# A gated attention and MLP mix on one Trainium2 core: the last product of the second half in seven parts, and three weight quarters copied in DRAM

## The chip, the cores and the metric

The kernel runs on one core of a Trainium2 chip. The time is device microseconds of one execution; three runs of the kernel before are given. A profiled execution gives the trace: TensorE is called PE (its weight loads PEld), VectorE DVE, ScalarE ACT, GpSimd POOL, SyncE SP. SP and POOL issue nearly all DMAs.

## What is computed

The input x has 2048 rows of 1024. Two branches are mixed by a gate (cut from the reference):

```
g = sigmoid((x * gate_w).sum(-1, keepdims=True))
a = attention(x, wqkv) @ wo              # 32 heads of 32, each position sees 8 positions at a step of 2 backwards
b = (gelu(x @ w_gate) * (x @ w_up)) @ w_down     # inner width 3584
out = g * a + (1 - g) * b
```

Both output products are one in the kernel: the attention's result (1024 wide, already scaled by g) and h = gelu(..)*(..) (3584 wide) stand side by side, 4608 wide, and w_down and wo stand below each other. That "down" product, 2048 x 4608 times 4608 x 1024, is what the change touches.

## The kernel before

**The first 513 us.** The projections of x run as units of 28 matmuls of 128x512 (about 6.05 us each, lines 340 to 410); unit numbers run from 0 to 77, and functions hung on a unit with `at(unit, fn)` are issued when it begins. Beside the units, VectorE does the attention and the sums that the units need. Each pair of columns of w_gate and w_up is loaded by SP (L166, `load_pair`) some three units before use, and summed by VectorE (L322). Results go to DRAM: h (`h_d`, L259), the attention's result (`o_d`, L774), both issued by POOL. Units 36 to 53 (`NQKV + 10` is 36), of which the change speaks, run from about 263 to 372 us.

**The down product.** It runs in two halves of 1024 rows, `down(0)` and `down(1)`. Within a half, the left matrix A and the right matrix R are cut in 2x2 quarters, and the product is done with seven products of quarters and sums (a Strassen-Winograd scheme). A quarter is [128, 18, 512]: 18 slices of 128 of the inner dimension (`NK`), 512 columns. The seven products, in the order in which they run: A11·R11, A12·R21, S·T1, S2·T2 (S2 = A21 + A22 - A11), AD·T3, A22·T4, and last A12·R22, where A12 has become A12 - S2. Here these are products 1, 2, 5, 6, 7, 4 and "the last". The sums T1 to T4 of R's quarters are made early (`t_forms`, L862) and lie in DRAM as `t_d`, in load sequence: each partition's 18 KB in one run. R11, R21 and R22 are loaded straight from w_down and wo (`load_R`, L829), in runs of 512 columns, 1 KB.

**One product** is done in one of two ways. Plain (`mm`, L1062): four row blocks j of 128, 18 matmuls each of 128x512, 72 in all. Or in seven again (`level2`, L1037): both quarters are cut in 2x2, and seven inner products of 18 matmuls of 128x256 give 126. For that VectorE makes four sums of A's parts (`forms_L`, L995) and four of R's (`forms_R`, L1003), each 128x2304; ScalarE copies between PSUM parts as inner products end (L1042); ScalarE zeroes the left halves of the banks first (`zero_left`, L1015); VectorE adds the third inner product to the right halves at the end (`join`, L1022). Of a set of four banks, the left halves of the first two are final after the second inner product, the right halves of the last two after the fifth and the join, the right halves of the first two after the sixth and the join, the left halves of the last two after the seventh. In the second half product 1 and products 5, 6, 7, 4 are done in seven; A12·R21 and the last are plain. In the second half R's sums for products 5, 7 and 4 come from the first half through DRAM (`r_d`, `load_F`).

PSUM's eight banks are two sets of four, `XT` and `VT`, used in turn. `u2` and `qs` are running totals in SBUF. `add_out` (L1071) adds a total to a bank and stores the 128x512 result: POOL issues the stores, only those of the last product in the second half are SP's (L1067). Six output tiles are used in rotation.

**What sets the order.** Each engine runs its instructions in the order of the program. Ten buffers of one quarter each are assigned by hand in `plan`; a load waits until the last reader of its buffer is done. SP issues the loads in order, and a DMA also waits for the landing of the eighth DMA before it on the same queue, whose semaphore it shares. SP's order in the second half: A11, R11, A12, A21, R21, A22, T1, r_d, T2, T3, r_d, T4, r_d, R22.

The end of the second half before the change, from line 1160 on:

```
            level2(XT, A22, B["T4"], B["L4"], B["R4"])
            joins(XT, B["R4"])
            for j in range(4):
                add_out(XP[j], u2[:, j, :], 1, 0, j)
...
            for j in range(4):
                mm(VP[j], A12, B["R22"], j, True)
...
                add_out(VP[j], qs[:, j, :], 0, 1, j)
```

Of the kernel before, what the change touches and what calls it, by code (L numbers as in the profile page):

```python
# [9 lines left out]
ALU = mybir.AluOpType  # L10
BF16 = mybir.dt.bfloat16
# [4 lines left out]
P = 128  # L16
SC = 512
# [51 lines left out]
def kernel(  # L69
# [12 lines left out]
    nc = tc.nc  # L82
# [4 lines left out]
    o2 = out.rearrange("b s d -> (b s) d")  # L87
# [4 lines left out]
    NK = NPAIR + NT // 2  # L92
# [10 lines left out]
    def reg(kb, n):  # L103
        o = int(kb * KB)
        return arena[:, o:o + n]

    def reg3(kb, a, b):
        return reg(kb, a * b).rearrange("p (a b) -> p a b", a=a)
# [4 lines left out]
    def regf(kb, n):  # L113
        return reg(kb, 2 * n).bitcast(F32)
# [3 lines left out]
    def bank(i):  # L118
        return banks[:, i, :]
# [6 lines left out]
    o_d = [[tc.dram_tile([P, NT, SC], BF16, name=f"o_d{s}{c}") for c in range(2)] for s in range(2)]  # L126
    t_d = [tc.dram_tile([P, NK, SC], BF16, name=f"t_d{k}") for k in range(4)]
    r_d = {k: tc.dram_tile([P, 3 * (NK // 2) * (SC // 2)], BF16, name=f"r_d{k}") for k in (1, 3, 4)}
    z_d = tc.dram_tile([HK, S], F32, name="z_d")
    g_d = tc.dram_tile([2, S], BF16, name="g_d")  # L130
    w_d = tc.dram_tile([NBLK, 32, NJ, SC], BF16, name="w_d")
# [2 lines left out]
    TT = V.tensor_tensor  # L134

    with tc.manual_schedule(engines={mybir.EngineType.PE, mybir.EngineType.DVE, mybir.EngineType.Activation,
# [42 lines left out]
        for s in range(2):  # L179
            b0 = R_X[s]  # L180
            f = XF()
# [6 lines left out]
            f.T4 = reg3(b0 + 24, HK, SC)  # L188
            f.T3 = f.R12
            xf.append(f)  # L190

        def flat(a):
            return a.rearrange("p a b -> p (a b)")
# [7 lines left out]
        def x_form3(s):  # L201
            f = xf[s]
            TT(out=flat(f.T3), in0=flat(f.R22), in1=flat(f.R12), op=ALU.subtract)

# [154 lines left out]
        class Unit:  # L359
# [37 lines left out]
            def p73(self):  # L397
                f = self.f
                self.mm(self.Y, "S3", f.T3, False)
                self.mm(self.Z, "S4", f.R22, False)  # L400
# [78 lines left out]
        def at(n, fn):  # L479
            hooks.setdefault(n, []).append(fn)  # L480
# [77 lines left out]
        NQKV = len(units)  # L558
# [259 lines left out]
        def r_parts(half, nh, i0=0, i1=NK):  # L818
            ns = slice(nh * SC, (nh + 1) * SC)
            if i0 < NH_:  # L820
                e = min(i1, NH_)
                yield slice(i0, e), B_w_down[:, ns].rearrange("(i two p) n -> p i two n", two=2, p=P)[:, i0:e, half, :]
            if i1 > NH_:
                a = max(i0, NH_)
                yield slice(a, i1), A_wo[:, ns].rearrange("(p t) n -> p t n", t=NT)[:, 4 * half + a - NH_:4 * half + i1 - NH_, :]

        def load_R(b, half, nh, i0=0, i1=NK):
            for sl, src in r_parts(half, nh, i0, i1):
                nc.sync.dma_start(out=b[:, sl, :], in_=src)  # L829

        def load_T(b, k):
            nc.sync.dma_start(out=b, in_=t_d[k - 1][:])
# [41 lines left out]
        def tf_close():  # L874
            while tf_q[0] < N1:
# [7 lines left out]
        plan = [dict(A11=4, R11=5, A12=2, R21=7, A21=6, A22=3, T1=1, T2=9, S=8, AD=0, L5=4, R5=5, L6=7, R6=1,  # L883
                     T3=8, L7=4, R7=5, T4=9, L4=1, R4=7, R22=6),
                dict(A11=0, R11=4, L1=5, R1=8, A12=3, A21=9, R21=1, A22=7, T1=2, AD=6, S=0, T2=8, L5=4, R5=5, L6=1, R6=2,
                     T3=0, L7=4, R7=5, T4=8, L4=2, R4=1, R22=9)]
        u2 = regf(R_U2, 4 * SC).rearrange("p (j n) -> p j n", j=4)
        qs = regf(R_QS, 4 * SC).rearrange("p (j n) -> p j n", j=4)
        on = [0]

        def out_tile():
            k = on[0] % 6
            on[0] += 1
            return reg(R_OUT[k], SC) if k < 4 else omgrep[:, (k - 4) * SC:(k - 3) * SC]
# [23 lines left out]
        def run(*gens):  # L918
            for g in gens:
                for _ in g:  # L920
                    pass
# [52 lines left out]
        KH, HN = NK // 2, SC // 2  # L974
# [9 lines left out]
        def quarter(b, kh, h):  # L984
            return b[:, kh * KH:(kh + 1) * KH, h * HN:(h + 1) * HN]

        def quads(b):
            return flat(b).rearrange("p (f k n) -> p f k n", f=4, k=KH)

        def forms_L(f, b):  # L990
            f = quads(f)
            q = lambda kh, h: quarter(b, kh, h)
            for o_, a, b_, op in ((f[:, 0], q(0, 1), q(1, 1), ALU.add), (f[:, 1], f[:, 0], q(0, 0), ALU.subtract),
                                  (f[:, 2], q(0, 0), q(0, 1), ALU.subtract), (f[:, 3], q(1, 0), f[:, 1], ALU.subtract)):
                TT(out=o_, in0=a, in1=b_, op=op)  # L995
                yield 1.3

        def forms_R(f, b):
            f = quads(f)
            q = lambda kh, h: quarter(b, kh, h)  # L1000
            for o_, a, b_, op in ((f[:, 0], q(0, 1), q(0, 0), ALU.subtract), (f[:, 1], q(1, 1), f[:, 0], ALU.subtract),
                                  (q(0, 1), q(1, 1), q(0, 1), ALU.subtract), (f[:, 2], q(1, 0), f[:, 1], ALU.subtract)):
                TT(out=o_, in0=a, in1=b_, op=op)  # L1003
                yield 1.3

        def woven(*gens):
            for cs in zip(*gens):
                yield from cs

        def two_banks(bk, i, h):  # L1010
            return banks[:, bk[2 * i]:bk[2 * i] + 2, h * HN:(h + 1) * HN]

        def zero_left(bk):
            for i in range(2):
                nc.scalar.activation(out=two_banks(bk, i, 0), in_=omgrep[:, SUP:SUP + SC].rearrange("p (a b) -> p a b", a=2),  # L1015
                                     func=ACT.Copy, scale=0.0)
# [4 lines left out]
        def join(bk, rf, i):  # L1021
            TT(out=two_banks(bk, i, 1), in0=two_banks(bk, i, 1), in1=part5(rf), op=ALU.add)  # L1022
# [5 lines left out]
        def level2(bk, L, R, lf, rf, mid=None):  # L1028
            p5d = part5(rf)
            lf, rf = quads(lf), quads(rf)  # L1030
            lq, rq = lambda r, c: quarter(L, c, r), lambda r, c: quarter(R, r, c)
            c = lambda i, h, j: banks[:, bk[2 * i + j], h * HN:(h + 1) * HN]

            def prod(i, h, l, r, then=None):
                for j in range(2):
                    for kt in range(KH):
                        nc.tensor.matmul(c(i, h, j), lhsT=l[:, kt, j * P:(j + 1) * P], rhs=r[:, kt, :], start=False,  # L1037
                                         stop=(kt == KH - 1), skip_group_check=True)
                    if then:
                        then(j)  # L1040

            cp = lambda d, s_: nc.scalar.copy(out=d, in_=s_)  # L1042
            prod(0, 0, lq(0, 0), rq(0, 0), lambda j: cp(c(1, 1, j), c(0, 0, j)))
            prod(0, 0, lq(0, 1), rq(1, 0))
            prod(1, 0, lf[:, 0], rf[:, 0], lambda j: cp(p5d[:, j, :], c(1, 0, j)))
            prod(1, 1, lf[:, 1], rf[:, 1], lambda j: cp(c(0, 1, j), c(1, 1, j)))
            prod(1, 1, lf[:, 2], rq(0, 1), lambda j: cp(c(1, 0, j), c(1, 1, j)))
            if mid:
                mid()
            prod(0, 1, lf[:, 3], rq(1, 1))  # L1050
            prod(1, 0, lq(1, 1), rf[:, 2])

        def down(s):
            B = Bs(s)
            last = s == 1
            eng = nc.gpsimd
            base = s * SUP
            XT, VT = (6, 7, 0, 1), (2, 3, 4, 5)

            def mm(ps, L, R, j, start, q0=0, q1=NK):  # L1060
                for q, i in list(enumerate(KORD))[q0:q1]:
                    nc.tensor.matmul(ps, lhsT=L[:, i, j * P:(j + 1) * P], rhs=R[:, i, :], start=(start and q == 0),  # L1062
                                     stop=(q == NK - 1), skip_group_check=not start)
# [5 lines left out]
            def add_out(ps, t_, c, nh, j):  # L1069
                ot = out_tile()  # L1070
                TT(out=ot, in0=ps, in1=t_, op=ALU.add)  # L1071
                emit(ot, c, nh, j)

            A11, A12, A21, A22, S, AD = (B[k] for k in ("A11", "A12", "A21", "A22", "S", "AD"))
            XP = [bank(XT[j]) for j in range(4)]
            VP = [bank(VT[j]) for j in range(4)]
# [44 lines left out]
            def mid6():  # L1121
                for j in range(4):
                    nc.scalar.copy(out=qs[:, j, :], in_=VP[j])
                zero_left(VT)
                loads(s, "T3")

# [8 lines left out]
            else:  # L1135
                loads(s, "T4", "R22")
                rest = woven(forms_L(B["L7"], AD), forms_R(B["R7"], B["T3"]))
                take(rest, 4)
# [20 lines left out]
            for j in range(4):  # L1159
# [1 line left out]
                    join(VT, B["R7"], j // 2)  # L1161
                add_out(VP[j], qs[:, j, :], 1, 1, j)
                TT(out=u2[:, j, :], in0=VP[j], in1=u2[:, j, :], op=ALU.add)
            level2(XT, A22, B["T4"], B["L4"], B["R4"])
            joins(XT, B["R4"])
            for j in range(4):
                add_out(XP[j], u2[:, j, :], 1, 0, j)
            if not last:
# [1 line left out]
                zero_left(XT)  # L1170
                N = Bs(1)
                rest = pieces(scale_task(N["A11"], 1, 0, 0, NE_), woven(forms_L(N["L1"], N["A11"]), forms_R(N["R1"], N["R11"])))
            for j in range(4):
                mm(VP[j], A12, B["R22"], j, True)
                if not last:
                    take(rest, 3)
                add_out(VP[j], qs[:, j, :], 0, 1, j)
            if not last:
                run(rest)
                loads(1, "T1")  # L1180

# [79 lines left out]
```

## Time and profile before

| | |
|---|---|
| three runs, us | 724.71, 722.42, 722.99 (median 722.99) |
| profiled execution, us | 723.03, of which the span is 721.2 |
| granted TensorE clock | 0.999 |
| PE busy | 709.4 us, 98% of the span, 3995 records |
| PEld, DVE, ACT, POOL busy | 403.7, 661.8, 324.9, 123.8 us |
| matmuls of 128x512 by `mm` (L1062) | 352 records, 78.1 us |
| matmuls of 128x256 by `level2` (L1037) | 1134 records, 124.6 us |
| DMA | 153.17 MB, mean 212 GB/s |
| loads of R from w_down (L829) | six of 1792 KB, median 18.3 us to landing |
| loads of T (L832) | eight of 2304 KB, median 12.7 us to landing |

Matmuls overlap, so the mean duration of one (379 ns, 273 ns) is longer than its share of the row; durations below are taken from the distance between starts or from the chain of waits. Some matmul records are missing from the trace. "Idle before" in a timeline is the engine's wait, with what ended it. DMA share 1 means that all 16 DMA engines moved packets all the time; shares a little over 1 come from overlapping packets.

### The profile page before, as it was taken

Reading aid. Unit: us, or ns where it says so; the run is one execution under the profiler, and the core shown is the slowest. Engines: PE = TensorE matmul, PEld = TensorE weight load, DVE = VectorE, ACT = ScalarE, POOL = GpSimd, SP = SyncE. Lnnn points to the kernel's source line nnn. Section 1 sums busy time; section 2 is a strip of 40 time slices with the busy share of each in tenths; the row PEclk is TensorE's granted clock in tenths of the full one; section 3 lists DMA queues with packets and bytes.
Section 4 is the critical chain, followed back from the end, with each engine's and each line's share of the span. In section 5 each row is a group of like instructions: output and inputs, shape, how many; then the busy total and the mean of one; then the engine's idle time right before and its main releaser. Section 6 shows DMA issues by size and latency. Waiting matters only on the chain. (4 is left out here: it accounts for less than half of the span.)

```text
span 721.2 us, 10603 instructions
## 1 busy us (share of the span) xinstructions
PE 709.4 (98%) x3995; PEld 403.7 (56%) x4053; DVE 661.8 (92%) x711; ACT 324.9 (45%) x590; POOL 123.8 (17%) x218
## 2 busy tenths in 40 slices
PE   8999999999999999999999999999999999999997
PEld 4466656655544444444444444444447885758883
DVE  2699989999999999999999999999989998999972
ACT  4454546444456665555555555555222321232410
POOL 1323544133210310000010101000211013010011
PEclk9999999999999999999999999999999999999999
DMA  9966643278264746251644846371994699994941
GB/s 274 285 182 217 228 141 132 100 246 304 98 208 130 234 144 201 92 174 59 205 137 128 279 150 215 98 284 60 325 410 154 234 389 404 397 427 195 361 135 58
DMA packets 102450, 153.17 MB, mean 212 GB/s; under 512 B 18976, under 2 KB 81856, under 8 KB 99584
## 3 DMA queue, kind: packets, MB, share of 16 engines
q1 hardware_dynamic: 87280, 103.69, 42.9%
q0 software_dynamic: 14832, 48.29, 18.9%
q8 instruction: 31, 0.51, 0.3%
q10 hardware_dynamic: 288, 0.52, 0.2%
q14 instruction: 19, 0.16, 0.1%
HBM read 103.32 MB, written 47.06 MB: 209 GB/s over the span
## 5 line engine op out<-in xcount | busy, mean ns | idle before, releaser
L365 PE MATMUL banks<-arena 128*128 128x512 bf16 x2136 | 472.1, 379 | 4.2 <-DVE arena L402 0.7
L365 PEld LDWEIGHTS <-arena 128*128 128x128 bf16 x2184 | 240.5, 111 | 235.2 <-issue 7.0
L1037 PE MATMUL banks<-arena 128*128 128x256 bf16 x1134 | 124.6, 273 | 0.0
L1037 PEld LDWEIGHTS <-arena 128*128 128x128 bf16 x1134 | 111.0, 98 | 13.8 <-issue 0.3
L402 DVE TENSOR_TENSOR arena<-banks,arena 128x1024 bf16<-128x1024 f32 x78 | 95.1, 1220 | 13.0 <-PE banks L365 7.4
L388 ACT COPY arena<-banks 128x512 f32<-128x512 f32 x78 | 45.8, 587 | 130.8 <-PE banks L365 130.8
L1062 PE MATMUL banks<-arena 128*128 128x512 bf16 x352 | 78.1, 379 | 1.4 <-DMA arena<-in_B_w_down_dram 1.0
L373 ACT CAST arena<-banks 128x512 bf16<-128x512 f32 x102 | 59.7, 585 | 42.4 <-PE banks L365 42.4
L744 DVE TENSOR_TENSOR arena<-arena 128x2048 bf16<-128x2048 bf16 x64 | 76.9, 1218 | 0.5
L597 DVE TENSOR_TENSOR arena<-arena 128x2048 bf16<-128x2048 bf16 x64 | 74.6, 1217 | 0.1
L751 DVE TENSOR_TENSOR arena<-arena 128x2048 bf16<-128x2048 bf16 (+2 forms) x96 | 73.8, 774 | 1.0
L259 POOL DMA_DIRECT2D h_d<-arena x28 | 20.2, 723 | 243.2 <-DVE arena L253 199.9
L1062 PEld LDWEIGHTS <-arena 128*128 128x128 bf16 x360 | 35.1, 98 | 43.1 <-DVE banks L1022 1.3
L395 ACT COPY banks<-banks 128x512 f32<-128x512 f32 x78 | 44.5, 570 | 21.8 <-PE banks L365 20.0
L383 ACT COPY banks<-banks 128x512 f32<-128x512 f32 x78 | 44.9, 576 | 13.6 <-PE banks L365 12.1
L995 DVE TENSOR_TENSOR arena<-arena 128x2304 bf16<-128x2304 bf16 x36 | 47.8, 1350 | 0.5
L1042 ACT COPY banks<-banks 128x256 f32<-128x256 f32 x54 | 19.2, 356 | 54.9 <-PE banks L1037 54.7
L915 DVE TENSOR_TENSOR arena<-arena 128x2048 bf16<-128x2048 bf16 (+1 forms) x40 | 41.7, 1109 | 0.0
L371 ACT ACTIVATE arena<-banks 128x512 bf16<-128x512 f32 x54 | 32.2, 597 | 15.4 <-PE banks L365 15.3
L322 DVE TENSOR_TENSOR arena<-arena 128x1024 bf16<-128x1024 bf16 x60 | 38.6, 685 | 0.5
L253 DVE TENSOR_TENSOR arena<-arena 128x2048 bf16<-128x2048 bf16 x28 | 34.0, 1214 | 1.9 <-ACT arena L250 1.4
L1003 DVE TENSOR_TENSOR arena<-arena 128x2304 bf16<-128x2304 bf16 x24 | 32.2, 1348 | 2.2 <-DMA arena<-t_d 2.0
(90 smaller groups left out, 422.7 us busy)
## 6 DMA issues: line engine op xcount, KB each, us to landing
arena<-t_d SPq DMA_DIRECT2D x8, 2304.0 KB, 12.7
h_d<-arena POOLq DMA_DIRECT2D x28, 512.0 KB, 4.2
arena<-in_B_w_down_dram SPq DMA_DIRECT2D x6, 1792.0 KB, 18.3
t_d<-arena POOLq DMA_DIRECT2D x36, 256.0 KB, 4.0
arena<-h_d SPq DMA_DIRECT2D x6, 1536.0 KB, 11.5
arena<-in_B_w_gate_dram SPq DMA_DIRECT2D x15, 512.0 KB, 5.6
arena<-in_B_w_up_dram SPq DMA_DIRECT2D x15, 512.0 KB, 4.4
arena<-in_B_w_down_dram SPq DMA_DIRECT2D x28, 256.0 KB, 6.9
```

Source lines behind the costliest of these rows:

```text
L365: self.pe = nc.tensor.matmul(ps, lhsT=self.L[form](kt), rhs=rhs[:, kt, :], start=(start and kt == 0), stop=(kt == HK - 1), skip_group_chec ...
L373: nc.scalar.copy(out=o_, in_=i_)
L383: nc.scalar.copy(out=self.Y, in_=self.X)
L388: nc.scalar.copy(out=self.p5s, in_=self.V)
L395: nc.scalar.copy(out=self.Z, in_=self.Y)
L402: TT(out=self.T[:, :, c2s], in0=pair, in1=self.p5s.rearrange("p (o n) -> p o n", o=1).to_broadcast([P, 2, SC]), op=ALU.add)
L597: TT(out=dst, in0=q.rearrange("p (o s) -> p o s", o=1).to_broadcast([P, NWIN, AC]), in1=_win_ap(k, [[-DIL, NWIN], [1, AC]]), op=ALU.mult)
L744: TT(out=prod2[(t // 2) % 2][:, t % 2], in0=ab, in1=_win_ap(v[:, t, HALO:HALO + AC], [[SJ, NJ], [-DIL, NWIN], [1, SJ]]), op=ALU.mult)
L751: TT(out=out_, in0=h(0), in1=h(1), op=ALU.add)
L995: TT(out=o_, in0=a, in1=b_, op=op)
L1037: nc.tensor.matmul(c(i, h, j), lhsT=l[:, kt, j * P:(j + 1) * P], rhs=r[:, kt, :], start=False, stop=(kt == KH - 1), skip_group_check=True)
L1062: nc.tensor.matmul(ps, lhsT=L[:, i, j * P:(j + 1) * P], rhs=R[:, i, :], start=(start and q == 0), stop=(q == NK - 1), skip_group_check=not ...
```

## The change

The last product of the second half is done in seven (`level2`) instead of plain. Its sums of A12 and R22 go to buffers 4 and 5 (`L3`, `R3`, new in the plan) and stand in VectorE's order behind the outputs of product 7 and ahead of the joins of product 4; the zeroing of its banks stands inside product 4. Its outputs are summed by halves of 256 columns, as parts of the banks become final, in six stretches with the two joins between them; SP stores them as they are complete: three stores of 512 columns and two of 256. `o2` is the output.

The three quarters R11, R21, R22 of the stacked weights are copied from DRAM to DRAM by POOL into `w_c`, in load sequence, three slices at a time, one such copy at the start of each of 18 units; all loads of R (three in each half) then read `w_c`, in two parts of 1152 KB, instead of w_down (1792 KB) and wo (512 KB).

```diff
+    w_c = {k: tc.dram_tile([P, NK, SC], BF16, name=f"w_c{k[0]}{k[1]}") for k in ((0, 0), (1, 0), (1, 1))}
...
-        def load_R(b, half, nh, i0=0, i1=NK):
-            for sl, src in r_parts(half, nh, i0, i1):
-                nc.sync.dma_start(out=b[:, sl, :], in_=src)
+        def load_R(b, half, nh):
+            for i0 in range(0, NK, NK // 2):
+                sl = slice(i0, i0 + NK // 2)
+                nc.sync.dma_start(out=b[:, sl, :], in_=w_c[half, nh][:, sl, :])
+
+        def lay_out(k, i0):
+            for sl, src in r_parts(*k, i0, i0 + 3):
+                nc.gpsimd.dma_start(out=w_c[k][:, sl, :], in_=src)
+
+        for m_, k_ in enumerate(w_c):
+            for e_, i_ in enumerate(range(0, NK, 3)):
+                at(NQKV + 10 + 6 * m_ + e_, lambda k_=k_, i_=i_: lay_out(k_, i_))
...
-                     T3=0, L7=4, R7=5, T4=8, L4=2, R4=1, R22=9)]
+                     T3=0, L7=4, R7=5, T4=8, L4=2, R4=1, R22=9, L3=4, R3=5)]
...
-            level2(XT, A22, B["T4"], B["L4"], B["R4"])
+            if last:
+                run(woven(forms_L(B["L3"], A12), forms_R(B["R3"], B["R22"])))
+            level2(XT, A22, B["T4"], B["L4"], B["R4"], last and (lambda: zero_left(VT)))
...
-            for j in range(4):
-                mm(VP[j], A12, B["R22"], j, True)
-                if not last:
+            if last:
+                level2(VT, A12, B["R22"], B["L3"], B["R3"])
+                ots = [out_tile() for _ in range(4)]
+
+                def half_out(j, h, store=()):
+                    hs = slice(h * HN, (h + 1) * HN)
+                    TT(out=ots[j][:, hs], in0=VP[j][:, hs], in1=qs[:, j, hs], op=ALU.add)
+                    for a, z in store:
+                        nc.sync.dma_start(out=o2[base + j * P:base + (j + 1) * P, SC + a:SC + z], in_=ots[j][:, a:z])
+
+                half_out(0, 0)
+                half_out(1, 0)
+                join(VT, B["R3"], 1)
+                half_out(2, 1)
+                half_out(3, 1, [(HN, SC)])
+                join(VT, B["R3"], 0)
+                half_out(0, 1, [(0, SC)])
+                half_out(1, 1, [(0, SC)])
+                half_out(2, 0, [(0, SC)])
+                half_out(3, 0, [(0, HN)])
+            else:
+                for j in range(4):
+                    mm(VP[j], A12, B["R22"], j, True)
...
```

More of the change, by code (lines that the diff above doesn't have):

```diff
@@ L1172, in down @@
                 rest = pieces(scale_task(N["A11"], 1, 0, 0, NE_), woven(forms_L(N["L1"], N["A11"]), forms_R(N["R1"], N["R11"])))
-            for j in range(4):
-                mm(VP[j], A12, B["R22"], j, True)
-                if not last:
+            if last:
[19 more added lines that the diff above has]
+                    mm(VP[j], A12, B["R22"], j, True)
                     take(rest, 3)
-                add_out(VP[j], qs[:, j, :], 0, 1, j)
-            if not last:
+                    add_out(VP[j], qs[:, j, :], 0, 1, j)
                 run(rest)
```

## The prediction

> **What bounds the kernel now.** I read the share of busy time first, then the chain that ended last, then TensorE's waits, then the stage around each edit. TensorE is busy 709.4 us of 721.2 at a granted clock of 0.999, so only what shortens its row of matmuls or its few gaps counts. The end of the chain of waits:
>
> ```profile
> 589.12 21.95 DMA arena<-in_B_w_down_dram
> ...
> 611.15 19.52 DMA arena<-in_B_w_down_dram
> 630.67 0.14 issue
> 630.80 0.38 PE banks L1062
> ...
> 646.50 55.17 PE banks L1037 x504
> 701.68 0.21 PE banks L1062
> ...
> 717.25 0.69 DVE arena L1071
> ```
>
> The columns are start, length, what. The last product, A12·R22, starts at 701.68 and its matmuls end at 717.23; then come one VectorE sum (to 717.94), its store, and the end of the span at 721.23. The two DMA pieces are the loads of R11 and R21; R21 lands at 630.67, and TensorE waits for it:
>
> ```profile
> PE banks L1062 <- DMA arena<-in_B_w_down_dram: 1.0, 1, 1.0
> ```
>
> (Waiter, releaser, us in total, times, longest.) That is TensorE's only wait for memory behind the start. Next, the stretches of 10 us (columns: PE, PEld, DVE, ACT, POOL busy; granted clock; DMA share; GB/s):
>
> ```profile
> 620.00:630.00 10.00, 9.78 (x90) 8.51 (x88) 8.67 (x10) 3.25 (x8) 1.08 (x2) 1.00 1.06 374
> 640.00:650.00 10.00, 9.95 (x63) 5.97 (x62) 9.93 (x10) 2.81 (x6) 1.27 (x3) 1.00 1.02 433
> 660.00:670.00 10.00, 10.00 (x94) 8.96 (x93) 9.90 (x10) 2.53 (x7) 0.00 (x0) 1.00 0.87 343
> 680.00:690.00 10.00, 10.00 (x94) 8.95 (x92) 9.96 (x11) 3.27 (x9) 0.00 (x0) 1.00 1.03 375
> 690.00:700.00 10.00, 10.00 (x94) 8.97 (x93) 6.80 (x12) 2.46 (x7) 2.18 (x4) 1.00 0.21 72
> ```
>
> Two things are to be seen. The DMA engines are full around R21's landing, and move less (374, 375) where the column loads of R run than where only whole rows run (433). And VectorE has no room from 630 to 690, just as TensorE has none: what TensorE gains at 630.7 must be followed into VectorE's row.
>
> **The last product in seven.** It removes 72 matmuls of 128x512 that take 717.23 - 701.68 = 15.55 us, and adds 126 of 128x256. The 504 of the chain's 55.17 us are four such products, so one costs 13.79. On the path: **-1.76 us**.
>
> It adds eight sums of 128x2304 on VectorE. Six of that shape take 7.81 us (below), so eight take 10.4. They stand behind the last sum into `u2` (ends 696.69) and ahead of the joins and the four stores of product 4; before, VectorE stood idle there, 3.1 us and then 1.3. Queued behind them are those joins and outputs, and POOL, which stores them; TensorE waits for none of them.
>
> ```profile
> 646.34 55.34 PE L1037 MATMUL banks<-arena 128*128 128x256 bf16 x504
> ...
> 680.22 7.81 DVE L995 TENSOR_TENSOR arena<-arena 128x2304 bf16<-128x2304 bf16 x6
> ...
> 696.01 0.68 DVE L1163 TENSOR_TENSOR arena<-banks,arena 128x512 f32<-128x512 f32 x1
> ```
>
> Does TensorE wait for the sums? Each inner product is 18 matmuls, 1.97 us. The third (start 705.6) needs the first two sums, done at 699.3; the fourth (707.6) needs 701.9; the fifth (709.6) needs 704.5; the seventh (713.5) the last at 707.1. Six us of room: cost 0. R22 must be in SBUF at 698, not at 701.5: it is issued at 673.76, and the DMA rate drops to 72 GB/s in the stretch 690-700, so it has landed by about 692. The zeroing of the left halves by ScalarE needs 1.1 us, released at about 698.3 by its own copies, in time for 701.7. Cost 0; if it were not hidden, 1.1.
>
> VectorE's end, from durations of its rows (0.69 for 512 columns from PSUM, 1.22 for 1024 at L402; on that line 0.42 for 256, an estimate; a pitch of 0.6 between two of 0.69): sums to 707.1, two joins and four outputs 3.7, to 710.8, two half outputs to 711.6. The second join needs the fifth inner product (711.5) and ScalarE's copy of 0.36 behind it: 711.9 to 712.6. Two halves, 713.4; the other join behind the sixth product (713.5), 714.2; two halves, 715.0; one more, 715.4. TensorE ends at 701.68 + 13.79 = 715.47, so the last half output follows TensorE and not VectorE's own queue, with 0.1 us to spare. It takes 0.42 where 0.69 stood: **-0.27**. The last store is 64 KB, not 128. Between POOL's stores of 64 KB (2.3 us to landing) and 256 KB (2.6) lie 0.3 us, so 64 KB less gives **-0.1**; four stores within 2.5 us on SP (0.33 each to issue) could return up to 0.4. I take -0.1.
>
> **R11, R21, R22 through a copy.** The copies are 21 DMAs on POOL, one to two per unit, about 263 to 373 us. POOL is busy 9.1 of those 110 us; at 0.54 to 0.86 us for one of its issues (rows L865, L774) they add 11 to 18. Behind each in POOL's queue stands an h_d or o_d store, which is read 100 us later or more, and whose buffer comes round five units on. 7.1 MB read and written in 110 us are 64 GB/s each way; the stage moves 117 to 137 at a DMA share of 0.39 to 0.45. By those rows the share rises by 0.22, or by 0.44 if a byte read and a byte written both count: below 0.9 in either case. The loads that could feel it are the weight pairs:
>
> ```profile
> 299.72 0.37 SPq L166 DMA_DIRECT2D arena<-in_B_w_up_dram  x1
> ...
> 309.56 2.61 DVE L322 TENSOR_TENSOR arena<-arena 128x1024 bf16<-128x1024 bf16 x4
> ```
>
> Issued 299.72, landed 4.4 later (the page's median for that load), needed at 309.56: 5.4 us of room. VectorE's own operations show no trace of POOL's issues (L744: 1211 to 1226 ns in all 64). Cost 0.
>
> What it removes: a load of R is 2.36 MB; at 374 GB/s it takes 6.3 us, at 433 5.4. R11 and R21 both stand in the full stretch ahead of R21's landing, so it lands 1.7 us sooner or more, and SP, whose issue of R21 waits for the landing of R11's first part (611.07 and 611.15 in the chain), goes on sooner. The wait of 1.02 us at 630.8 is gone.
>
> **But little of it arrives.** VectorE is anchored to the end of the product before that wait (its join at 629.89 waits for TensorE) and runs without a gap until 696.7, so TensorE comes 1.02 us earlier to sums that come no earlier. The tightest: product 7 is the third of the four in the 504, and its fifth inner product, matmul 324 of the row, starts at 646.34 + 324 x 0.1095 = 681.81. It needs the first sum of the group at 680.22, which takes 1.35 (mean of L995): 681.57. That is 0.24 us of slack, some 0.04 of it the signal (the 0.05 pieces of issue in the chain). The same sum gives about 0.35 at two places of product 6. So the removed wait comes back in products 6 and 7 but for **-0.2**. Bounds: 0 and -1.02.
>
> A rule speaks against this part. The Trainium skill, "DMA: Bandwidth & Descriptors", section Specifications, gives 512 B as the smallest transfer for line rate; R's runs of 1 KB would then lose nothing. The rates of 374 and 433 above speak against it, though other traffic is mixed into both. By it this part would bring 0 instead of 0.2.
>
> **Sum**, against the profiled execution's 723.03 (span 721.23 and 1.80 around it; the median of the three is 722.99, so the sum holds for it too): -1.76 - 0.27 - 0.1 - 0.2 = -2.33, or **720.7**.
>
> **Rivals.**
> 1. The whole wait of 1.02 us comes back: if VectorE's row gets shorter too. For it: TensorE's one wait on DMA. Against: VectorE's 9.80 to 10.00 per 10 us. 719.9.
> 2. The end is VectorE's or a store's, not TensorE's. The third and fourth output tiles of the last product were stored just before by product 4, whose outputs the new sums delay to 709.0 and 709.6. At the page's median of 5.2 us from issue to landing they are free at 714.5 and 715.1, not at about 712, and VectorE's queue (two halves, join, four halves, 3.5 us) ends 1.1 to 1.9 later. Against: those medians come from the full stretch; the DMA rate is 66 GB/s here. 722.0.
> 3. R21 lands no sooner: runs of 1 KB are already at the rate of long ones, or the order of SP's waits sets the landing. The wait stays. 720.9. The rule above says the same.
> 4. Slower. The copies fill the DMA engines, and the weight pairs miss their sums. In the full stage a load of 512 KB lands late:
>
> ```profile
> arena<-o_d SPq DMA_DIRECT2D x8, 512.0 KB, 11.5
> ```
>
> At 11.5 instead of 4.4 the sums are 1.7 us late in each of the four pairs loaded beside the copies (issues at 275.5, 299.7, 323.9, 348.1), VectorE is full there (108.0 of 110 us) and cannot catch up: +6.8, 727.5. It decides from a landing of 9.8 us, a DMA share near 1. Against: 0.45 plus at most 0.44.
>
> That the split doesn't happen is excluded by the order of TensorE's instructions: 54 more matmuls, all at the end, the rest unchanged.
>
> **Chances.** Forecast 0.52, rivals 0.13, 0.17, 0.13, 0.05. A difference of 0.3% (2.17 us, to 720.82) is about what a measurement of this kernel can tell from no change, and the forecast stands just beyond it: of its 0.52 I count 0.42 faster and 0.10 same. Faster 0.42 + 0.13 = 0.55; same 0.10 + 0.17 + 0.13 = 0.40; slower 0.05. The range runs from below rival 1 with a little more at the tail (719.3) to past rival 2 with the 0.4 of the stores (722.4).
>
> **What would show it.** After: no wait of TensorE for memory near 630; instead a wait for L1005's sums (today's L995) of about 0.8 us in products 6 and 7, above all near 680.9; 630 matmuls of 128x256 in a row; the last product 13.8 us; the last VectorE sum of 256 columns 0.4 us, released by TensorE. A wait of that sum's row for out_dram would show rival 2; VectorE waiting at the pairs' sums between 263 and 373 rival 4. The forecast is wrong most easily in the 0.2, where a tenth of a us of VectorE's pitch decides.

## The result, and the profile after

The changed kernel takes 726.0 us (median of 10 executions, 724.07 to 728.82); the kernel before 722.87 (10, 722.34 to 724.71). The ratio is 1.0046 with a 95% interval of [1.0028, 1.0064]: slower by 0.46%, where 720.7 was forecast, 0.3% faster. The profiled execution took 726.45 us, its span is 724.7.

TensorE's wait for R21 is gone, as forecast, and a longer wait for another engine stands in its place. The waits of TensorE in the changed kernel (waiter, releaser, us in total, times, longest), the first line:

```profile
PE banks L1072 <- ACT arena L1094: 3.4, 1, 3.4
```

TensorE's timeline (start, us, engine, line, operation, xcount, in brackets the idle time before and what ended it), its last two rows: product 2 of the second half, and the rest:

```profile
633.06 15.70 PE L1072 MATMUL banks<-arena 128*128 128x512 bf16 x72 [3.38 <-ACT arena L1094]
648.60 69.09 PE L1047 MATMUL banks<-arena 128*128 128x256 bf16 x630
```

Product 1 starts at 615.77, where it started at 615.86 before. Product 2 waits 3.38 us, not 1.02, and for ScalarE, not for R21. The last row has 630 matmuls as intended, and ends at 717.7. The chain that ended last shows where ScalarE's lateness comes from, and what stands behind the last matmul (start, length, what):

```profile
597.95 12.63 DMA out_dram<-omgrep
...
632.43 0.59 ACT arena L1094
...
633.06 15.70 PE banks L1072 x72
648.76 68.94 PE banks L1047 x630
...
717.80 0.71 DVE banks L1032
```

A store of one output tile, issued by POOL at 597.95, lands 12.63 us later. VectorE needs that tile. Its row around it:

```profile
609.45 0.69 DVE L1081 TENSOR_TENSOR omgrep<-banks,arena 128x512 bf16<-128x512 f32 x1 [5.68 <-DMA out_dram<-omgrep]
610.61 0.69 DVE L1081 TENSOR_TENSOR omgrep<-banks,arena 128x512 bf16<-128x512 f32 x1 [0.47 <-DMA out_dram<-omgrep]
...
627.16 4.63 DVE L916 TENSOR_TENSOR arena<-arena,omgrep 128x2048 bf16<-128x2048 bf16 x4
631.70 1.30 DVE L1032 TENSOR_TENSOR banks<-banks,arena 128x512 f32<-128x512 f32 x2
```

The same place in the kernel before, on VectorE:

```profile
606.10 1.29 DVE L1071 TENSOR_TENSOR omgrep<-banks,arena 128x512 bf16<-128x512 f32 x2 [2.25 <-DMA out_dram<-omgrep]
...
623.25 4.61 DVE L906 TENSOR_TENSOR arena<-arena,omgrep 128x2048 bf16<-128x2048 bf16 x4
...
629.89 0.70 DVE L1022 TENSOR_TENSOR banks<-banks,arena 128x512 f32<-128x512 f32 x1 [1.27 <-PE banks L1037]
```

One wait of 2.25 us has become two of 6.15 together. From there on VectorE's row is 3.9 us late (627.16 against 623.25). Before, it still reached the joins ahead of TensorE and waited there; now the joins come at 631.70, and behind them the ScalarE copies that product 2 needs.

The end of the kernel, VectorE's row in the changed kernel:

```profile
714.84 0.42 DVE L1191 TENSOR_TENSOR omgrep<-banks,arena 128x256 bf16<-128x256 f32 x1 [1.98 <-ACT banks L1052]
715.76 0.42 DVE L1191 TENSOR_TENSOR omgrep<-banks,arena 128x256 bf16<-128x256 f32 x1 [0.50 <-PE banks L1047]
717.80 0.70 DVE L1032 TENSOR_TENSOR banks<-banks,arena 128x512 f32<-128x512 f32 x1 [1.61 <-PE banks L1047]
718.53 0.76 DVE L1191 TENSOR_TENSOR arena<-banks,arena 128x256 bf16<-128x256 f32 x2
719.21 0.69 DVE L1032 TENSOR_TENSOR banks<-banks,arena 128x512 f32<-128x512 f32 x1
...
720.60 0.75 DVE L1191 TENSOR_TENSOR arena<-banks,arena 128x256 bf16<-128x256 f32 x2
```

The first two half outputs, put at 711.6 at the latest, end at 716.18. The join that the prediction put at 711.9 to 712.6 starts at 717.80, right behind TensorE's last matmul, and all the rest of the output stands behind it in VectorE's queue. From TensorE's end to VectorE's there are 3.6 us (717.71 to 721.35); before there were 0.71.

**The sum of the two profiled spans**, 724.7 - 721.2 = +3.5: the start of product 1 -0.1; the wait before product 2 3.38 - 1.02 = +2.4; the last product 13.8 instead of 15.55, -1.76; VectorE behind TensorE's end 3.63 - 0.71 = +2.9. That makes +3.4. So the gain was there, and two new costs of 2.4 and 2.9 took it back twice over. Product 4, the other products of the second half and the first 595 us are as before.

The stage with the copies is not among the costs. The stretch 300 to 350 of the kernel before, then of the changed one (us; PE, PEld, DVE, ACT, POOL busy; clock; DMA share; GB/s):

```profile
300.00:350.00 50.00, 49.74 (x228) 22.65 (x232) 49.24 (x56) 27.60 (x46) 4.57 (x6) 1.00 0.48 144
```

```profile
300.00:350.00 50.00, 50.00 (x234) 22.66 (x232) 49.25 (x56) 27.50 (x46) 11.08 (x15) 1.00 0.62 190
```

POOL is busy 6.5 us more, the DMA share rises by 0.14 and not by the 0.22 to 0.44 that were allowed for, and TensorE and VectorE are as full as before.

### The profile page after: what moved, and what is told of

It reads as the page before. It is cut to its first block, busy times and chain, and to the rows that moved or that the text cites. A ratio compares the mean times of both kernels' runs of the same rounds, so it can differ in the third digit from the quotient of the medians.

```text
span 724.7 us, 10828 instructions
## 1 busy us (share of the span) xinstructions
PE 710.6 (98%) x4107; PEld 409.0 (56%) x4107; DVE 673.4 (93%) x725; ACT 328.5 (45%) x600; POOL 138.8 (19%) x239
## 5 line engine op out<-in xcount | busy, mean ns | idle before, releaser
L366 PE MATMUL banks<-arena 128*128 128x512 bf16 x2184 | 474.8, 379 | 1.5 <-DVE arena L403 0.7
L366 PEld LDWEIGHTS <-arena 128*128 128x128 bf16 x2184 | 240.5, 111 | 235.2 <-issue 7.0
L1047 PE MATMUL banks<-arena 128*128 128x256 bf16 x1260 | 138.3, 273 | 0.0
L1047 PEld LDWEIGHTS <-arena 128*128 128x128 bf16 x1260 | 123.2, 98 | 15.3 <-issue 0.3
L1072 PE MATMUL banks<-arena 128*128 128x512 bf16 x288 | 62.8, 379 | 3.4 <-ACT arena L1094 3.4
L1005 DVE TENSOR_TENSOR arena<-arena 128x2304 bf16<-128x2304 bf16 x40 | 53.3, 1353 | 0.5
L1072 PEld LDWEIGHTS <-arena 128*128 128x128 bf16 x288 | 28.2, 98 | 37.1 <-issue 3.6
L1052 ACT COPY banks<-banks 128x256 f32<-128x256 f32 x60 | 21.4, 356 | 57.4 <-PE banks L1047 57.2
L1013 DVE TENSOR_TENSOR arena<-arena 128x2304 bf16<-128x2304 bf16 x28 | 37.7, 1353 | 0.2
```

Source lines behind the costliest of these rows:

```text
L366: self.pe = nc.tensor.matmul(ps, lhsT=self.L[form](kt), rhs=rhs[:, kt, :], start=(start and kt == 0), stop=(kt == HK - 1), skip_group_chec ...
```

## The experiments

Two theories stood after the result. **S**: the loads of R, whose packets have grown from 1 KB to 9 KB, take DMA time from POOL's stores, so an output tile comes free late. **J**: VectorE's sums wait not for the half of a PSUM bank that they read, but for matmuls that write elsewhere. Their rivals: one of the two carries the whole loss. All times are medians; ratios are to the kernel before on the same chip (722.74, 722.88 and 723.18 us in the three groups of runs).

**One part at a time.** The copies and `load_R` alone, on the kernel before:

```diff
+    w_c = {k: tc.dram_tile([P, NK, SC], BF16, name=f"w_c{k[0]}{k[1]}") for k in ((0, 0), (1, 0), (1, 1))}
...
+                nc.sync.dma_start(out=b[:, sl, :], in_=w_c[half, nh][:, sl, :])
```

> The copies alone, the last product plain as before. Theory S (the long packets of the copied quarters take DMA time from POOL's stores, VectorE waits for an output tile, TensorE waits 3.4 us near 632 instead of 1.0): 722.9 + 2.4 = 725.3, VectorE waits about 6 us for out_dram near 604 to 611. Rival C (that wait is chance of one execution, and the copies do what the prediction said): 722.7, no such wait.

Measured: 724.86 us, ratio 1.0035 [1.0020, 1.0051]. VectorE's wait came as expected (6.0, below); TensorE waits 1.99 us before product 2 in this profiled execution, less than the 3.4 expected. Then the split of the last product alone, with R loaded as before:

```diff
-    w_c = {k: tc.dram_tile([P, NK, SC], BF16, name=f"w_c{k[0]}{k[1]}") for k in ((0, 0), (1, 0), (1, 1))}
...
-                nc.sync.dma_start(out=b[:, sl, :], in_=w_c[half, nh][:, sl, :])
+            for sl, src in r_parts(half, nh, i0, i1):
+                nc.sync.dma_start(out=b[:, sl, :], in_=src)
```

> The split alone, R loaded as before. Theory J (the join of the last two banks waits for the seventh inner product, so join, two halves, join, four halves, 3.6 us, all stand behind TensorE's end, not 0.4): -1.76 + 2.9 = 1.15 slower than before, 724.0, and TensorE's wait near 630.8 stays at 1.0. If all of the loss were the split's: 726.0.

Measured: 723.92 us, ratio 1.0013 [1.0005, 1.0022]. Each part alone is slower, by 2.1 and 1.2 us; together 3.3, and the whole change costs 3.1. As far as the scatter lets one tell, the two losses add up. VectorE's waits between 575 and 640 (waiter, releaser, total, times, longest) with the copies alone:

```profile
DVE omgrep L1081 <- DMA out_dram<-omgrep: 6.0, 2, 5.3
```

and with the split alone:

```profile
DVE omgrep L1071 <- DMA out_dram<-omgrep: 2.1, 1, 2.1
```

The long wait for the output tile goes with the copies. With the split alone TensorE's last matmuls end at 715.1 and VectorE at 718.8: the long tail goes with the split.

**Which sums wait for what.** The whole change, but the joins are done bank by bank:

```diff
+                def join_bank(k):
+                    o_ = banks[:, VT[k], HN:SC]
+                    TT(out=o_, in0=o_, in1=part5(B["R3"])[:, k % 2, :], op=ALU.add)
...
-                join(VT, B["R3"], 1)
+                join_bank(2)
                 half_out(2, 1)
+                join_bank(3)
                 half_out(3, 1, [(HN, SC)])
```

and likewise for banks 0 and 1.

> The changed kernel with the joins of the last product done bank by bank (two sums of 256 columns for one of 2x256), copies as in the change. Theory J: VectorE starts both joins ahead of TensorE's end, the tail behind TensorE's end falls from 3.6 to about 0.5 us: 726.0 - 2.9 = 723.1. Rival Q (VectorE's own queue, with the eight sums ahead, sets the tail): 725.5 or more.

Measured: 727.37 us, ratio 1.0057 [1.0037, 1.0076]. The expectation of a shorter tail was missed. The row shows why; TensorE's seventh inner product runs here from 715.85 to 717.82:

```profile
716.94 0.43 DVE L1197 TENSOR_TENSOR banks<-banks,arena 128x256 f32<-128x256 f32 x1 [0.63 <-PE banks L1047]
...
717.92 0.43 DVE L1197 TENSOR_TENSOR banks<-banks,arena 128x256 f32<-128x256 f32 x1
```

The join of bank 2's right half, final since the fifth inner product, starts at 716.94: 0.1 after the ninth of the 18 matmuls of the seventh (715.85 + 0.98 = 716.83), the last that write bank 2, and into its left half. Bank 3's follows the eighteenth. So the wait goes by whole bank, whichever half is read, and that is J as it has to be put. Splitting the join into banks moves one join and its sum ahead of TensorE's end; eight instructions still stand behind it, as in the change, and from TensorE's end to VectorE's there are 3.25 us (717.82 to 721.07) instead of 3.6. The median of 727.37 (724.45 to 731.1) can't be told from the change's 726.0 with so much scatter.

**The output tile.** The whole change, with eight output tiles instead of six (the two new ones lie in buffers that are free by then):

```diff
-            k = on[0] % 6
+            k = on[0] % 8
...
+            if k == 6:
+                return gblk.rearrange("p a b -> p (a b)")
+            if k == 7:
+                return md.rearrange("p a b -> p (a b)").bitcast(BF16)
```

> The changed kernel with eight output tiles in rotation instead of six (two small buffers that are no longer read serve as tiles). Theory S: VectorE no longer waits for POOL's store near 604 to 611, is 6 us earlier, and TensorE's wait near 632 is gone: 726.0 - 3.4 = 722.6, with the long tail of 3.6 us still there. Rival (the wait near 632 comes from loads that land late): 726.0.

Measured: 723.99 us, ratio 1.0013 [1.0005, 1.0022]: 2.0 less than the change, where 3.4 was expected. TensorE's row:

```profile
629.46 15.70 PE L1076 MATMUL banks<-arena 128*128 128x512 bf16 x70
...
663.62 51.44 PE L1051 MATMUL banks<-arena 128*128 128x256 bf16 x468 [0.62 <-DVE arena L1017]
```

Product 2 follows product 1 with no wait at all, and 34 us later the wait stands before a sum of VectorE, in product 6. VectorE's wait for an output tile is 1.4 here. The copies with the tile cured (723.99) are worth as much as no copies (723.92): what they gain at R21 comes back on VectorE.

**The length of the runs.** The whole change, six tiles, but the copies are laid out by slices, so that R is read in runs of 1 KB as it was from the weights:

```diff
-    w_c = {k: tc.dram_tile([P, NK, SC], BF16, name=f"w_c{k[0]}{k[1]}") for k in ((0, 0), (1, 0), (1, 1))}
+    w_c = {k: tc.dram_tile([NK, P, SC], BF16, name=f"w_c{k[0]}{k[1]}") for k in ((0, 0), (1, 0), (1, 1))}
```

> The changed kernel, its copies laid out so that each load of R is again in runs of 1 KB (slices outermost in w_c), the rest as in the change. Theory S in the form that the length of a packet decides (loads and POOL's stores take turns packet by packet, so a store of 4 KB packets gets less beside packets of 9 KB than beside 1 KB): VectorE's wait for out_dram near 604 falls from 6 back to about 2.2 us, TensorE's wait near 632 from 3.4 to 1.0 or less; 726.0 - 2.3 = 723.7, with little scatter. Rival (SP issues the copied loads sooner, in any layout, and that crowds the store out): wait of 5 to 6, 726.

Measured: 724.09 us, ratio 1.0017 [1.0008, 1.0026]. VectorE's wait for the tile is back at 2.1; TensorE waits 0.86 for the copied R21 in place of 1.02 for w_down. The bytes, the queues and the order of the issues are those of the change; only the length of the runs differs, and the 2 us are gone. But the length of the runs also changes how long SP needs to issue. SP's issues of R11's two halves and of the first loads behind them, in the change:

```profile
589.24 1.65 SPq L831 DMA_DIRECT2D arena<-w_c  x2
599.77 0.86 SPq L815 DMA_DIRECT2D arena<-h_d  x2
```

and with runs of 1 KB:

```profile
587.56 13.16 SPq L831 DMA_DIRECT2D arena<-w_c  x2
600.82 6.24 SPq L815 DMA_DIRECT2D arena<-h_d  x2
```

With 1 KB the same issues take 13.16 and 6.24 us, so SP's later loads go out later, and that could spare the stores as well. This run alone does not separate the two. Between 1 and 9 KB, runs of 3 KB:

```diff
+    w_c = {k: tc.dram_tile([NK // 3, P, 3, SC], BF16, name=f"w_c{k[0]}{k[1]}") for k in ((0, 0), (1, 0), (1, 1))}
```

> The change whole, but the copies are laid out so that R11, R21 and R22 are read in runs of 3 KB, between the 9 KB of the change and the 1 KB of the run with runs of 1 KB. Theory S (the loads' packets and those of POOL's stores share the DMA engines packet by packet, so the longer packet takes the larger share): VectorE's wait for an output tile near 605 to 610 lies between the 2.1 us of 1 KB runs and the 6.1 of the change, about 3.5, and the time between 724.1 and 726.0, about 724.8. Rival (the length of the runs has a step, not a slope): the wait is one of the two, 2.1 or 6.1, and the time 724.1 or 726.0. The tail is that of the change, 3.6 us from TensorE's end to VectorE's.

Measured: 724.6 us, ratio 1.0022 [1.0012, 1.0033], with a wait for the tile of 2.6 in the profiled execution. The wait lies between, but nearer to 1 KB than the 3.5 that I expected. The interval of the time overlaps that of 1 KB and that of the change (four executions took 723.3 to 724.0, four 725.2 to 725.7), so how the loss grows between 1 and 9 KB stays open. This run does answer the question left above. SP issues here as fast as in the change:

```profile
588.30 1.16 SPq L831 DMA_DIRECT2D arena<-w_c  x2
599.86 1.08 SPq L815 DMA_DIRECT2D arena<-h_d  x2
```

POOL's store of the sums, which it issues just ahead of the tiles' stores, goes out at 594.37, and the loads behind R11 5.5 us later; with the copies alone it is 5.6 us (594.92 and 600.49). Yet the wait is 2.6 here and 6.0 there. So it is not SP's earlier issuing that holds the tile, and the length of the runs remains.

**A better tail.** The split without copies, and each bank touched only once it is whole: the right half's join, then the whole bank's sum and store, bank by bank:

```diff
+                level2(VT, A12, B["R22"], B["L3"], B["R3"])
+                for j in range(4):
+                    o_ = banks[:, VT[j], HN:SC]
+                    TT(out=o_, in0=o_, in1=part5(B["R3"])[:, j % 2, :], op=ALU.add)
+                    add_out(VP[j], qs[:, j, :], 0, 1, j)
```

> The split alone, R loaded as before; bank by bank in the order in which TensorE finishes the banks, VectorE adds the third inner product to the bank's right half and then the total to all 512 columns, and stores. Theory K (a VectorE sum on a bank waits for the last matmul into that bank, whichever half it reads): only the last bank's two sums, 0.35 + 0.69, stand behind TensorE's end, where before 0.69 did: -1.76 + 0.35 = 721.4. If VectorE's own queue sets the tail whatever the order: 723.9 as with the split alone.

Measured: 721.66 us, ratio 0.9983 [0.9973, 0.9993]. VectorE runs without a gap from 712.14 to 716.49 here, 1.5 us past TensorE's end at 714.98, so its own queue sets part of this tail. Then with the third inner product added to the running totals `qs` in SBUF, which wait for no bank, and only then the four sums:

```diff
+                for j in range(4):
+                    q_ = qs[:, j, HN:SC]
+                    TT(out=q_, in0=q_, in1=part5(B["R3"])[:, j % 2, :], op=ALU.add)
+                for j in range(4):
+                    add_out(VP[j], qs[:, j, :], 0, 1, j)
```

> The split alone, R loaded as before; VectorE adds the third inner product to the running total in SBUF while TensorE still works, and one sum of 512 columns per bank is left for the end, as before the change. Theory K: the tail is that of before, 0.7 us, and only TensorE's saving is left: -1.76, 721.0. TensorE's wait near 630 stays at 1.0. If the eight sums ahead of it make VectorE late: 722 or more.

Measured: 720.66 us (720.33 to 721.65), ratio 0.9968 [0.9956, 0.9980]. This beats both kernels. VectorE's end in it:

```profile
709.89 1.42 DVE L1179 TENSOR_TENSOR arena<-arena 128x256 f32<-128x256 f32 x4
...
715.21 0.69 DVE L1071 TENSOR_TENSOR arena<-banks,arena 128x512 bf16<-128x512 f32 x1 [0.29 <-PE banks L1037]
```

Each sum follows the last matmul into its bank, and the last starts 0.1 behind TensorE's end at 715.1. Behind TensorE there is one instruction of 0.69, as in the kernel before.

**What is left for the copies.** The same tail, with the copies and eight tiles:

> The copies of the change, eight output tiles and the tail with the totals prepared ahead. No wait of VectorE for out_dram of more than 1.5, no wait of TensorE near 630, instead 0.6 to 0.9 in products 6 and 7 on VectorE's sums, so the copies give at most 0.2 on top of the split: 720.8. If the wait of 1.0 came back whole: 720.0.

Measured: 720.86 us, ratio 0.9974 [0.9964, 0.9983]. No wait of TensorE at 630.56, and one of 0.35 for a sum of VectorE's in product 6, at 664.45; another of 0.89 stands at 581.3, in the first half. VectorE's wait for an output tile is 2.5 here, more than the 1.5 expected, but TensorE does not wait for it. With TensorE freed from the tile, no gain of the copies can be seen. Last, without copies, but R21 asked for ahead of A21:

```diff
-                loads(1, "A12", "A21", "R21", "A22")
+                loads(1, "A12", "R21", "A21", "A22")
```

> The version in which the early terms are added to the two free buffers first, without any copy in DRAM and with six output tiles (720.66 us), but R21 is asked for ahead of A21 instead of behind it. Theory (the 1.2 us that TensorE waits for R21 near 630.5 are to be had by the order of the loads, without copies, but come back on VectorE's sums in products 6 and 7, as in the runs with eight tiles): no wait for w_down near 630, 0.6 to 0.9 us on VectorE in products 6 and 7, time about 720.5. Rival 1, the whole wait comes back as time: 719.7. Rival 2, A21 or A22 now land too late for the sums that need them: 721 or more.

Measured: 725.08 us, ratio 1.0021 [1.0009, 1.0032]. My theory fell, and the second rival holds: VectorE waits for A21's rows of h_d, 4.1 us, and its joins and TensorE with it. VectorE's row, then TensorE's:

```profile
631.39 1.23 DVE L906 TENSOR_TENSOR arena<-arena,omgrep 128x2048 bf16<-128x2048 bf16 x1 [4.11 <-DMA arena<-h_d]
```

```profile
633.89 17.39 PE L1062 MATMUL banks<-arena 128*128 128x512 bf16 x72 [2.58 <-ACT arena L1084]
```

The row of 72 matmuls takes 17.39 here and 15.70 everywhere else; the last section comes back to it. Of the 5.1 us by which this span is longer than that of the version with R21 in its old place (724.1 against 719.0), 2.0 had arisen by product 1, nearly all in the first 11 us, at the loads of x and behind them, where executions differ; 1.4 is the longer wait, 1.7 the slower row.

## Why the prediction was wrong, step by step

**The last product in seven: right.** -1.76 was forecast; the row of 630 takes 69.09, five products of 13.8. The eight new sums, the zeroing and R22 cost nothing, as worked out. With a tail that fits (720.66), the split is worth 2.2 us, and the forecast of this part with its tail was -2.13. That these two agree so well is luck: that run's tail has 0.69 and not 0.42, and in its profiled execution product 1 starts 0.47 sooner than before (615.39 against 615.86). The -0.1 for the smaller last store is not seen: from VectorE's end to the end of the span there are 3.3 us in both kernels (717.94 to 721.2, 721.35 to 724.7).

**VectorE's end: wrong.** The step that failed is "The second join needs the fifth inner product (711.5) and ScalarE's copy of 0.36 behind it". It went by which half of the banks is final. The program waits by bank: the join covers banks 2 and 3, whose left halves the seventh inner product still writes, so it waited for 717.71. Two halves, the other join and four halves then stood behind it: 3.6 us after TensorE's end instead of 0.42. The term of -0.27 was +2.9. The first two half outputs show the same: their left halves are final after the second inner product, and they start at 714.84 and 715.76, right after the ninth and the eighteenth matmul of the sixth (713.77 to 715.74), which writes the right halves of those two banks. (The profile puts the first wait down to a ScalarE copy, but the last of those ended at 714.21.) The evidence was in the trace of before, in a line that the prediction used for something else: the join at 629.89 with "1.27 <-PE banks L1037" waits for the very end of product 1, its seventh inner product, though the half that it reads had been final since the fifth, two inner products of 1.97 earlier. I took it for an anchor of VectorE's row and did not ask why a join should wait that long. A term that rests on a part being final before the whole is worth looking up in the old trace: here the same operation was there, with its wait.

The Trainium skill, "PSUM — Partial Sum Buffer", section "PSUM bank collisions raise a hardware error", says that two engines must not be in the same bank on the same partitions at once, even at different columns, and that waits should go by bank and not by address. The traces agree as far as they go: in the runs above each sum that waits for TensorE starts within about 0.1 us after the last matmul into its bank.

**The copies' own cost: right.** Nothing between 263 and 373 (TensorE 50.00 of 50 in 300 to 350). Rival 4 looked for the harm there, and there was none.

**What the copies remove: right as far as it went.** R21's wait goes (no wait at 629.46 with eight tiles), and most of it comes back on VectorE's sums, as "But little of it arrives" had it, though not where it was looked for: TensorE waits in product 6 (0.62 with eight tiles, 0.35 with the new tail as well), for a sum of R's parts (L1017, L1003 in the kernel before), and nowhere in product 7 near 680.9. The remaining -0.2 can't be seen: 723.99 against 723.92, and 720.86 against 720.66.

**What the faster load displaces: not asked.** The step that failed is "The wait of 1.02 us at 630.8 is gone": the landing of R21 was followed to its readers, and no one else was followed who uses the DMA engines in those us. With it fell "VectorE is anchored to the end of the product before that wait": in the changed kernel the joins come at 631.70, behind TensorE, and not ahead of it. POOL's stores use the DMA engines there. The DMA view of 600 to 604, while R11 is loaded by SP (q1) and POOL (q0) stores sums for `r_d`, and outputs behind them; packets, MB, share of 16 engines. Before:

```profile
q0 software_dynamic: 121, 1.48, 86.6%
q1 hardware_dynamic: 127, 0.14, 9.6%
```

After:

```profile
q1 hardware_dynamic: 79, 0.61, 36.0%
q0 software_dynamic: 80, 1.08, 63.3%
```

Before, SP's queue moved 127 packets of 1 KB beside POOL's 121 and got a tenth of the engines; after, 79 beside 80, most of them nine times as long, and it got over a third. In these 4 us, with R11 and POOL's sums under way throughout, the two queues take turns packet by packet in both kernels, and the length of the packet sets the share. With runs of 3 KB SP's queue moved 138 packets to POOL's 137 and got 26.2%, with runs of 1 KB from the copy 161 to 160 and 11.9%. POOL's packets in the two kernels are 12 to 14 KB long on average: nearly all of these bytes are of one store, the 1728 KB of sums that POOL issues at 595.42 in the changed kernel, 1.3 us ahead of the first tile's store on the same queue. It lands after 12.6 us instead of 9.9, and the tiles' stores land behind it; whether they would fare better ahead of it was not tried. The stores issued between 595 and 612 (xcount, KB each, median us from issue to landing), before:

```profile
out_dram<-arena POOLq DMA_DIRECT2D x5, 128.0 KB, 5.6
...
out_dram<-omgrep POOLq DMA_DIRECT2D x4, 128.0 KB, 7.9
```

and after:

```profile
out_dram<-omgrep POOLq DMA_DIRECT2D x4, 128.0 KB, 9.7
out_dram<-arena POOLq DMA_DIRECT2D x4, 128.0 KB, 11.7
```

A sum on VectorE needs one of the six tiles that these stores empty, and the joins and TensorE wait behind it. That is the +2.4 of this execution. The trace of before showed the candidate: VectorE already waited 2.25 us there for an output tile, so every us more on the stores was a us more on VectorE, and little stood between VectorE and TensorE: the 1.27 us that the join at 629.89 waited, and the 1.02 of TensorE behind it. Rival 2 had the right mechanism, output tiles held by stores, but at the tail (709 to 715), where the DMA engines are nearly idle, and not at 604, where they are full. Its first sentence, that the end is VectorE's and not TensorE's, came true, but through the banks and not through the tiles.

The cause is shown: the loss goes with the copies (724.86 against 722.74), goes away with two more tiles, and goes away with runs of 1 KB; both cures end where the split alone does (723.99 and 724.09 against 723.92). The size is some 2 us by the medians and differs between executions: TensorE's wait before product 2 is 3.38 us in the change, 2.57 in the run with joins by bank and 1.99 with the copies alone. That the engines take turns by packets is read from the counts above. The Trainium skill, "DMA: Bandwidth & Descriptors", section "Queues, rings and completion order", says that each DMA engine goes round its queues one packet at a time; the counts (127 to 121, 79 to 80, 138 to 137, 161 to 160) agree.

**The 512 B** of the Trainium skill ("DMA: Bandwidth & Descriptors", section Specifications), which the prediction weighed: with runs of 9 KB all traffic of the stretch from 597 to 612 together moved 428 GB/s, with 3 KB 420, with 1 KB 402, each at a share just above 1. So longer runs moved more here, against the rule as I put it, though the stretch holds other traffic too; yet in time the rule's outcome was the right one, since the faster landing was worth nothing.

## What to carry to other kernels

Where a change makes one transfer faster in a stretch in which the DMA engines are full, list the other queues' transfers in that stretch and who waits for their landing. Here what one queue gained another lost, and longer packets got a larger share. Before counting on a part of a PSUM bank that is final early, look in the old trace for what an operation on such a part waits for; here it was the last matmul into any part of the bank, and the cure was to do the early part's arithmetic in SBUF and touch each bank once. And a queue with a wait at its head costs everything behind it: seven instructions stood behind one join.

## What the runs showed of the hardware

One wait of TensorE cost more than its length. In the run with R21 asked for first, TensorE waited 2.58 us, started at 633.89, and then ran for some 3.4 us at half clock (granted 0.84 from 634.5 to 635, 0.50 to 638, 0.74 to 638.5, then 1.00). The stretch 635 to 638 of that run (us; PE, PEld, DVE, ACT, POOL busy; granted clock; DMA share; GB/s):

```profile
635.00:638.00 3.00, 3.00 (x8) 1.06 (x7) 3.00 (x3) 1.32 (x3) 0.00 (x0) 0.50 1.07 427
```

That is the 17.39 - 15.70 = 1.69 us above. The changed kernel's profiled execution waited longer, 3.38 us, and kept a clock of 1.00, as did the 2.57 us of the run with joins by bank; so the length of the wait alone does not decide whether the clock falls. The Trainium skill, "TensorE: Matmul & The Clock Gate", section "Part 1: The HAM clock gate", describes an activity window of 3.4 us that runs freely, and a halved clock after an idle one; the 3.4 us at 0.50 agree, and a wait shorter than that window was enough here. A halved clock may also be why the changed kernel's executions lie as far apart as 724.07 to 728.82: the four with a mean clock of 0.994 or 0.995 took 726.9 to 728.8, the six with 0.997 or 0.998 took 724.1 to 726.5. With the copies alone, the seven with 0.999 or 1.000 took 723.3 to 725.0, the five with 0.997 or 0.998 took 725.6 to 728.7. Nearly all of those executions have no trace, so this is argued, not shown; how much of the 2 us is the wait itself and how much a slower clock behind it stays open.
